# Attention backward loop: attention output two units later, and one VectorE multiply that empties two blocks' accumulators

## The chip, the cores and the metric

The kernel runs on one core of a Trainium2 chip. A core has five engines with queues of their own: TensorE (PE in the profile, with its weight loads as PEld), VectorE (DVE), ScalarE (ACT), GpSimd (POOL) and SyncE (SP). Each runs its instructions in program order and waits on semaphores for what other engines made. Matmuls write PSUM. VectorE and ScalarE empty PSUM in this kernel, and GpSimd works from SBUF to SBUF. The metric is the device time of one launch in microseconds, lower is better.

## The reference

Two attention blocks work on 2048 tokens of width 448, in bf16, and their outputs are concatenated. The kernel computes the outputs and the gradients of all eight inputs for a given `grad_out`. Block A is linear attention. Block B, which the change touches, is attention with 16 heads of width 28 that share one key and one value head:

```python
q = (x @ wq).reshape(B, S, H, Dh).transpose(0, 2, 1, 3)
k = x @ wk
v = x @ wv
scores = einsum("bhqd,bkd->bhqk", q, k) * (Dh ** -0.5)
p = softmax(scores, axis=-1)
o = einsum("bhqk,bkd->bhqd", p, v)
b = o.transpose(0, 2, 1, 3).reshape(B, S, H * Dh) @ wo
```

For block B the backward pass needs, per head and per query, the weighted sum of values o divided by the softmax denominator, the row sum D of dO * o, the gradient of the scores dS = p * (dP - D), and from that dQ = dS k, dK = dS^T q and dV = p^T dO.

## The kernel before

Phase A (about the first 195 us) computes everything of block A, and a short phase projects q, k and v of block B. The rest is one software-pipelined loop over units `u`, from 0 to 539, written out with `tc.manual_schedule()`: each engine executes exactly what the text of the loop issues to it, in that order.

A block `b` (64 of them) is a pair of heads and 256 queries. It takes 8 units, each of which handles 256 keys. Unit `u` belongs to block `u // 8`; "phase" below is `u % 8`. `due(u, lag)` gives the block whose first unit lies `lag` units back, or nothing if `u - lag` is no multiple of 8, so a step with lag 10 runs once per block, at phase 2. In unit `u`:

- `rows_SD` (PE): transposed scores S of unit `u` into two of the three PSUM banks `SB` and dP of unit `w = u - 16` into the two banks `DB`. In odd units the order of the matmuls is S0 S1 D0 D1 S0 S1 D0 D1 (0 and 1 are the heads), in even units S0 S1 D0 S0 S1 D0 D1 D1.
- The third bank of `SB` is `spare` in that unit. `onat_T` and `don_T` (PE transposes) and the output projection use it, and it is the bank that S0 of the next unit writes.
- ACT: `exp` of head 0 (L924), a copy `cp` of dP of head 1 to SBUF (L938), `exp` of head 1 (L970).
- DVE: dS of head 0 (L936, out of PSUM), then what is due of the steps below, and at the end of the unit a 32x32-block transpose of the dS of unit `u - 18` (L1003).
- POOL: dS of head 1 (L939, from `cp`), then what is due. In four of eight blocks it also makes two q staging copies `qst` (L832, phases 6 and 7).
- PE again: odd units do dK (`dk_m`); even units do `o_dq`, which adds two units' share of o (`o_mm`) and of dQ (`dq_mm`) into the bank `oq`, and then the dV groups (`dv_mm`) that are due.

In `oq` the rows 0 to 63 hold o with the softmax denominator of one block, and the rows 64 to 127 hold dQ of an older one. The steps for one block before the change:

| lag (phase) | engine | line | what |
|---|---|---|---|
| 2 to 8 | PE | 656 | `o_mm` into `oq[0:64]` |
| 9 (1) | DVE | 952 | copy of `oq[0:64]` to `oTs[0:64]`, f32 |
| 10 (2) | PE | 790 | `onat_T`: o back to query rows, into `spare` |
| 10 (2) | DVE | 799, 800 | reciprocal of the denominator; normalised o, into `oTs[:, 0:128]` |
| 10 (2) | POOL | 804, 807, 808 | `prod` = dO * o; `don` = dO / denominator; normalised o into `do_nat` in place of dO |
| 12 (4) | DVE, POOL | 812, 813 | `row_D`: row sums of `prod`, into a column of `don` |
| 14 (6) | PE, DVE | 821, 828 | `don_T` into `spare`, copy to `doT` for the dP of units 16 and later |
| 20 to 26 (4, 4, 6, 2) | PE | 656 | `dv_mm`, four groups |
| 27 (3) | DVE | 955 | dQ: `oq[64:128]` times `scale` into `qT_B` as bf16 |

Since `spare` is the next unit's S0 bank, S0 of the next unit waits for the VectorE instruction that reads `spare` last: L800 at phase 2, L828 at phase 6. The normalised o rows leave through a DMA transpose (`oTq`, SP queue, five times) and the output projections in `outs`, of which there is one per block at phase 0.

## Time and profile before

| what | value |
|---|---|
| median of three runs | 1067.29 us (1066.14 to 1067.74) |
| span of the profiled execution | 1064.7 us; its own device time is not listed beside it, the three runs lie 1.4 to 3.0 us above the span |
| loop, first to last `cp` start | 238.7 to 1015.0 us |
| granted TensorE clock | 0.999 |
| busy share of the span | PE 96%, DVE 84%, ACT 82%, POOL 73% |
| busy share from 300 to 400 us | PE 96%, DVE 98%, ACT 99%, POOL 90% |
| L939 POOL dS | 512 times, mean 1156 ns |
| L936 DVE dS, L1003 DVE transpose | 512 times each, mean 667 and 699 ns |
| L924, L938, L970 ACT | 512 times each, mean 612, 617 and 629 ns |
| L952 DVE copy, L955 DVE dQ | 64 times each, median 406 and 427 ns |

Busy times of DVE and ACT contain the overlap of an instruction with the one behind it: the tail of one runs beside the start of the next. For sums the distance from start to start in a stretch without waits is the better number. The three ACT instructions of a unit, for example, start 0.48 us apart where nothing holds them, so ACT needs 1.43 us for a unit.

### The profile page before, as it was taken

Reading aid. Unit: us, or ns where it says so; the run is one execution under the profiler, and the core shown is the slowest. Engines: PE = TensorE matmul, PEld = TensorE weight load, DVE = VectorE, ACT = ScalarE, POOL = GpSimd, SP = SyncE. Lnnn points to the kernel's source line nnn. Section 1 sums busy time; section 2 is a strip of 40 time slices with the busy share of each in tenths; the row PEclk is TensorE's granted clock in tenths of the full one; section 3 lists DMA queues with packets and bytes.
Section 4 is the critical chain, followed back from the end, with each engine's and each line's share of the span. In section 5 each row is a group of like instructions: output and inputs, shape, how many; then the busy total and the mean of one; then the engine's idle time right before and its main releaser. Section 6 shows DMA issues by size and latency. Waiting matters only on the chain.

```text
span 1064.7 us, 40036 instructions
## 1 busy us (share of the span) xinstructions
PE 1023.1 (96%) x16241; PEld 489.1 (46%) x16241; DVE 899.5 (84%) x1797; ACT 870.4 (82%) x1741; POOL 780.7 (73%) x1033
## 2 busy tenths in 40 slices
PE   9999999998999999999999999999999999999998
PEld 5555455434444444444444444444444444444444
DVE  7887400459999999999999999999999999999942
ACT  6463222489999999999999999999999999999522
POOL 6001242218888898899889989988998999888881
PEclk9999999999999999999999999999999999999999
DMA  9849899079999999999999999999999999999963
GB/s 264 167 108 192 171 203 246 22 137 181 193 188 196 182 203 189 188 202 191 197 181 197 181 196 195 193 189 194 196 197 192 199 190 183 208 190 177 222 141 89
DMA packets 689937, 195.15 MB, mean 183 GB/s; under 512 B 670616, under 2 KB 687792, under 8 KB 689752
## 3 DMA queue, kind: packets, MB, share of 16 engines
q1 hardware_dynamic: 680152, 179.92, 99.6%
q0 software_dynamic: 4640, 8.71, 2.9%
q10 hardware_dynamic: 4960, 3.96, 1.3%
q8 instruction: 127, 2.08, 0.8%
q14 instruction: 58, 0.48, 0.2%
HBM read 12.60 MB, written 10.84 MB: 22 GB/s over the span
## 4 chain that ended last, share of the span: by engine, by line
PE 43%; ACT 32%; issue 14%; POOL 5%; DVE 4%; DMA 1%; ACTq 0%; DVEq 0%; POOLq 0%
ACT cp L938 16%; PE agen L81 14%; ACT eT L970 13%; PE agen L656 10%; PE aacc L656 10%; PE aacc L81 5%; POOL dsT L939 3%; PE aacc L790 2%; ACT eT L924 2%; PE aacc L821 1%; DVE dsT L936 1%; DVE dsx L1003 1%; DMA out_dram<-dsT 1%; POOL eT L754 1%; POOL out_dram L778 0%
## 5 line engine op out<-in xcount | busy, mean ns | idle before, releaser
L939 POOL TENSOR_TENSOR dsT<-cp,eT 128x512 bf16<-128x512 bf16 x512 | 587.9, 1156 | 78.9 <-ACT cp L938 71.7
L1003 DVE STREAM_TRANSPOSE dsx<-dsT 128x512 f32<-128x512 f32 x512 | 357.6, 699 | 2.9 <-POOL dsT L939 0.8
L656 PEld LDWEIGHTS <-R 32*128 32x128 bf16 (+1 forms) x9104 | 227.9, 94 | 274.1 <-issue 238.4
L936 DVE TENSOR_TENSOR dsT<-agen,eT 128x512 bf16<-128x512 f32 x512 | 341.7, 667 | 10.9 <-PE agen L656 5.6
L938 ACT ACTIVATE cp<-agen 128x512 bf16<-128x512 f32 x512 | 315.8, 617 | 12.3 <-PE agen L656 11.2
L924 ACT ACTIVATE eT<-aacc 128x512 bf16<-128x512 f32 x512 | 313.6, 612 | 14.8 <-PE agen L656 4.8
L970 ACT ACTIVATE eT<-aacc 128x512 bf16<-128x512 f32 x512 | 322.2, 629 | 0.0
L656 PE MATMUL agen<-dsx,qX 32*32 32x512 bf16 x4096 | 267.6, 375 | 0.0
L656 PE MATMUL agen<-doT,R 32*128 32x256 bf16 x2048 | 247.1, 269 | 3.4 <-DVE dsT L936 1.4
L656 PE MATMUL aacc<-R,R 32*128 32x256 bf16 (+1 forms) x2240 | 218.2, 268 | 7.2 <-DVE oTs L800 2.5
L656 PE MATMUL agen<-eT,R 128*32 128x256 bf16 x2048 | 157.5, 274 | 0.1
L656 PE MATMUL agen<-dsT,R 128*32 128x256 bf16 x2048 | 156.8, 274 | 0.1
L656 PEld LDWEIGHTS <-qX 32*32 32x32 bf16 x4096 | 79.8, 89 | 113.7 <-issue 53.3
L656 PE MATMUL aacc<-eN,don 128*32 128x512 bf16 x1024 | 97.1, 379 | 0.1
L81 PEld LDWEIGHTS <-R 128*128 128x128 bf16 (+1 forms) x517 | 40.8, 98 | 43.5 <-issue 11.5
L406 POOL COPY pk<-R 128x256 bf16<-128x256 bf16 x4 | 1.6, 397 | 73.8 <-DVE R L366 73.7
L81 PE MATMUL agen<-R,R 128*128 128x448 bf16 (+1 forms) x180 | 42.1, 361 | 0.6 <-ACT R L225 0.6
L832 POOL COPY qst<-R 128x512 bf16<-128x512 bf16 x56 | 34.2, 611 | 4.0 <-DMA qX<-qst 3.9
L656 PEld LDWEIGHTS <-don 128*32 128x32 bf16 x1024 | 33.8, 97 | 1.4 <-issue 1.0
L804 POOL TENSOR_TENSOR prod<-R,oTs 128x128 f32<-128x128 bf16 x64 | 27.6, 431 | 9.3 <-DVE oTs L800 9.3
L422 DVE TENSOR_TENSOR osb<-aacc,pr 64x448 bf16<-64x448 f32 x2 | 1.2, 618 | 38.3 <-DMA out_dram<-osb 24.4
L955 DVE TENSOR_SCALAR R<-agen 64x256 bf16<-64x256 f32 x64 | 27.3, 427 | 3.6 <-PE agen L656 1.6
(231 smaller groups left out, 967.8 us busy)
## 6 DMA issues: line engine op xcount, KB each, us to landing
out_dram<-osb ACTq DMA_DIRECT2D x22, 112.0 KB
eN<-eT SPq DMA_TRANSPOSE x128
xa<-in_A_x_dram SPq DMA_DIRECT2D x8, 224.0 KB
ga<-in_grad_out_dram SPq DMA_DIRECT2D x4, 448.0 KB
xa<-in_grad_out_dram POOLq DMA_DIRECT2D x4, 448.0 KB, 6.1
out_dram<-wdq POOLq DMA_DIRECT2D x8, 224.0 KB, 4.0
eT<-in_grad_out_dram SPq DMA_DIRECT2D x4, 448.0 KB
eT<-in_B_x_dram SPq DMA_DIRECT2D x4, 448.0 KB
```

The lines of the kernel that those rows point to most:

```text
L81: nc.tensor.matmul(out_ap, lhsT=lhsT, rhs=rhs, start=start, stop=stop, tile_position=(0, 0))
L656: nc.tensor.matmul(out, lhsT=lhsT, rhs=rhs, start=start, stop=stop, tile_position=pos, skip_group_check=True)
L790: nc.tensor.transpose(onp[:, qb, :, :].rearrange("p h c -> p (h c)"), oTs[0:64, qb * P:(qb + 1) * P], identF[0:64, 0:64], tile_position=(0 ...
L804: nc.gpsimd.tensor_tensor(out=prod[b][:], in0=dnv, in1=os_, op=ALU.mult)
L832: eng.tensor_copy(out=st.rearrange("p (b s) a j -> p b s a j", s=2)[:, :, s, :, :], in_=src.unsqueeze(2).to_broadcast([P, 4, 4, 32]))
L924: nc.scalar.activation(out=eT(u)[:, 0, :], in_=sp[0][:, :], func=ACT.Exp, scale=scale)
L936: nc.vector.tensor_tensor(out=dst[:, 0, :], in0=dp[0][:, :], in1=ew[:, 0, :], op=ALU.mult)
L938: nc.scalar.activation(out=cp[:, :], in_=dp[1][:, :], func=ACT.Copy)
L939: nc.gpsimd.tensor_tensor(out=dst[:, 1, :], in0=cp[:, :], in1=ew[:, 1, :], op=ALU.mult)
L955: nc.vector.tensor_scalar(out=qT_B[g][64 * hp:64 * hp + 64, qc * 256:(qc + 1) * 256], in0=oq[64:128, 0:256], scalar1=scale, scalar2=None, ...
L970: nc.scalar.activation(out=eT(u)[:, 1, :], in_=sp[1][:, :], func=ACT.Exp, scale=scale)
L1003: nc.vector.transpose(out=dsx[b][:, tp, :, :, :].rearrange("p h t c -> p (h t c)").bitcast(F32), in_=dsT[y][:, :, :].rearrange("p h c -> p ...
```

## The change

Seven edits belong together.

1. `o_mm` works on units `u - 4` and `u - 3` instead of `u - 2` and `u - 1`, so o of a block is complete at lag 10 instead of 8, when dQ of the block two earlier is complete as well.
2. One VectorE `tensor_scalar` at phase 3 reads all 128 rows of `oq` and writes `oTs` in f32. Its per-row factor `fac` is 1 for the rows of o and `scale` for the rows of dQ. The row halves of o and dQ swap with the parity of the block. It takes the place of L952 and L955. GpSimd then casts the dQ half of `oTs` to bf16 into `qT_B`. In the last two blocks, where there is no o, dQ is taken as before.
3. `onat_T` and `o_norm` run at lag 12 instead of 10; the normalised o has a tile of its own, `o_s`.
4. `row_D` runs at lag 13 instead of 12, and stands behind L936 on DVE, and before the dS multiply of that unit on GpSimd.
5. The cast of the normalised o into `do_nat` becomes `o_keep`, at lag 14, and the DMA transpose with it.
6. The first `dv_mm` group goes from lag 20 to lag 18; `don` has two buffers instead of three.
7. `identF` shrinks to 64 columns and is copied from `identB`; the output projections from unit 456 on come 8 units later; the one clearing of `oTs` at unit 7 covers 128 rows instead of 64.

```diff
-        identF = pp_.tile([P, P], F32, name="identF", bufs=1)
-        make_identity(nc, identF[:])
+        identF = pp_.tile([P, 64], F32, name="identF", bufs=1)
+        for n in range(2):
+            nc.gpsimd.tensor_copy(out=identF[64 * n:64 * n + 64, :], in_=identB[64 * n:64 * n + 64, 64 * n:64 * n + 64])
         oTs = pp_.tile([P, 256], F32, name="oTs", bufs=1)
+        o_s = pp_.tile([P, 2, 2, 32], F32, name="o_s", bufs=1)
+        fac = pp_.tile([P, 2], F32, name="fac", bufs=1)
...
-        outs.update({456 + 8 * n: (10 + n // 2, n % 2 * (D // 2), (n % 2 + 1) * (D // 2)) for n in range(8)})
+        outs.update({464 + 8 * n: (10 + n // 2, n % 2 * (D // 2), (n % 2 + 1) * (D // 2)) for n in range(8)})
...
         def onat_T(b, bank):
+            r = 64 * (1 - b % 2)
             for qb in range(2):
-                nc.tensor.transpose(onp[:, qb, :, :].rearrange("p h c -> p (h c)"), oTs[0:64, qb * P:(qb + 1) * P],
-                                    identF[0:64, 0:64], tile_position=(0, 0))
+                nc.tensor.transpose(onp[:, qb, :, :].rearrange("p h c -> p (h c)"), oTs[r:r + 64, qb * P:(qb + 1) * P],
+                                    identF[r:r + 64, :], tile_position=(r, 0))
...
         def o_norm(b):
-            os_ = oTs[:, 0:P].rearrange("p (q h c) -> p q h c", q=2, h=2)
+            os_ = o_s[:]
...
-            dn = pw_.tile([P, 2, 2, 32], BF16, name="don", bufs=3)
+            dn = pw_.tile([P, 2, 2, 32], BF16, name="don", bufs=2)
...
-            nc.gpsimd.tensor_copy(out=dnv, in_=os_)
+            o_nat[b] = dnv, os_
+
+        def o_keep(b):
+            nc.gpsimd.tensor_copy(out=o_nat[b][0], in_=o_nat.pop(b)[1])
...
-                if (b := due(u, 10)) is not None:
+                if (b := due(u, 12)) is not None:
                     onat_T(b, spare)
...
                     nc.scalar.activation(out=cp[:, :], in_=dp[1][:, :], func=ACT.Copy)
+                    if (b := due(u, 13)) is not None:
+                        row_D(b)
                     nc.gpsimd.tensor_tensor(out=dst[:, 1, :], in0=cp[:, :], in1=ew[:, 1, :], op=ALU.mult)
...
+                if u % 8 == 3 and 0 <= (b := (u - 11) // 8) < NB + 2:
+                    r = 64 * (1 - b % 2)
+                    rr = slice(r, r + 64) if b < 2 else slice(0, P)
+                    if b < NB:
+                        nc.vector.tensor_scalar(out=oTs[rr, :], in0=oq[rr, 0:256], scalar1=fac[rr, b % 2:b % 2 + 1],
+                                                scalar2=None, op0=ALU.mult)
+                    if b >= 2:
+                        qc, pair, g, hp = blk(b - 2)
+                        rq = slice(64 * hp, 64 * hp + 64)
+                        if b < NB:
+                            nc.gpsimd.tensor_copy(out=qT_B[g][rq, qc * 256:(qc + 1) * 256], in_=oTs[rq, :])
...
                 if (b := due(u, 12)) is not None:
-                    row_D(b)
-                if (b := due(u, 9)) is not None:
-                    nc.vector.tensor_copy(out=oTs[0:64, :], in_=oq[0:64, 0:256])
-                if (b := due(u, 27)) is not None:
-                    qc, pair, g, hp = blk(b)
-                    nc.vector.tensor_scalar(out=qT_B[g][64 * hp:64 * hp + 64, qc * 256:(qc + 1) * 256],
-                                            in0=oq[64:128, 0:256], scalar1=scale, scalar2=None, op0=ALU.mult)
-                if (b := due(u, 10)) is not None:
                     o_norm(b)
+                if (b := due(u, 14)) is not None:
+                    o_keep(b)
...
-                    o_dq((u - 2, u - 1), (u - 20, u - 19))
-                    b, n = divmod(u - 20, 8)
-                    for k in {0: (0, 1), 2: (2,), 6: (3,)}.get(n, ()) if 0 <= b < NB else ():
-                        dv_mm(dv_acc, b, k // 2, k % 2)
+                    o_dq((u - 4, u - 3), (u - 20, u - 19))
+                    for k, lag in enumerate((18, 20, 22, 26)):
+                        if (b := due(u, lag)) is not None:
+                            dv_mm(dv_acc, b, k // 2, k % 2)
```

More of the change, by code (lines that the diff above doesn't have):

```diff
@@ L689 @@
         qst = pp_.tile([P, 8, 4, 32], BF16, name="qst", bufs=1)[:, :, :, :]
-        identF = pp_.tile([P, P], F32, name="identF", bufs=1)
-        make_identity(nc, identF[:])
+        identF = pp_.tile([P, 64], F32, name="identF", bufs=1)
+        for n in range(2):
+            nc.gpsimd.tensor_copy(out=identF[64 * n:64 * n + 64, :], in_=identB[64 * n:64 * n + 64, 64 * n:64 * n + 64])
         oTs = pp_.tile([P, 256], F32, name="oTs", bufs=1)
+        o_s = pp_.tile([P, 2, 2, 32], F32, name="o_s", bufs=1)
+        fac = pp_.tile([P, 2], F32, name="fac", bufs=1)
+        nc.gpsimd.memset(fac[:, :], 1.0)
+        for n in range(2):
+            nc.gpsimd.memset(fac[64 * n:64 * n + 64, n:n + 1], scale)
         wo = pc_.tile([P, 4, D], BF16, name="wo", bufs=1)
@@ L780 @@
         GW = [0, 0, 4, 4, 10, 10, 16, 16, 22, 22, 28, 28, 34, 34, 40, 40, 48, 48, 56, 56, 64, 64]
-        onps, tps2 = {}, {}
+        onps, tps2, o_nat = {}, {}, {}
         def due(u, lag):
@@ L853, in o_mm @@
                 for h in range(2):
-                    mmt(oq[32 * h:32 * h + 32, 0:256], vaug[:, t, :],
-                        eT(v)[:, h, t2 * 256:(t2 + 1) * 256], (0, 32 * h), t == 0, t == 15)
+                    r = 64 * (1 - b % 2) + 32 * h
+                    mmt(oq[r:r + 32, 0:256], vaug[:, t, :],
+                        eT(v)[:, h, t2 * 256:(t2 + 1) * 256], (0, r), t == 0, t == 15)
                 yield
@@ L862, in dq_mm @@
                 for h in range(2):
-                    mmt(oq[64 + 32 * h:96 + 32 * h, 0:256], kn[:, t, :],
-                        dsT[y][:, h, t2 * 256:(t2 + 1) * 256], (0, 64 + 32 * h), t == 0, t == 15)
+                    r = 64 * (b % 2) + 32 * h
+                    mmt(oq[r:r + 32, 0:256], kn[:, t, :],
+                        dsT[y][:, h, t2 * 256:(t2 + 1) * 256], (0, r), t == 0, t == 15)
                 yield
@@ L938 @@
                     nc.scalar.activation(out=cp[:, :], in_=dp[1][:, :], func=ACT.Copy)
+                    if (b := due(u, 13)) is not None:
+                        row_D(b)
                     nc.gpsimd.tensor_tensor(out=dst[:, 1, :], in0=cp[:, :], in1=ew[:, 1, :], op=ALU.mult)
+                if (b := due(u, 13)) is not None and not hasD:
+                    row_D(b)
                 gq, iq = divmod(u % 64 - 30, 8)
@@ L946 @@
                         qc_copy(nc.gpsimd, qst, qq, gq, iq)
-                if (b := due(u, 12)) is not None:
-                    row_D(b)
-                if u == 7:
-                    nc.vector.memset(oTs[64:128, :], 0.0)
-                if (b := due(u, 9)) is not None:
-                    nc.vector.tensor_copy(out=oTs[0:64, :], in_=oq[0:64, 0:256])
-                if (b := due(u, 27)) is not None:
-                    qc, pair, g, hp = blk(b)
-                    nc.vector.tensor_scalar(out=qT_B[g][64 * hp:64 * hp + 64, qc * 256:(qc + 1) * 256],
-                                            in0=oq[64:128, 0:256], scalar1=scale, scalar2=None, op0=ALU.mult)
-                if (b := due(u, 10)) is not None:
+                if u == 7:
+                    nc.vector.memset(oTs[:, :], 0.0)
+                if u % 8 == 3 and 0 <= (b := (u - 11) // 8) < NB + 2:
[9 more added lines that the diff above has]
+                            nc.gpsimd.tensor_copy(out=qT_B[g][rq, qc * 256:(qc + 1) * 256], in_=oTs[rq, :])
+                        else:
+                            nc.vector.tensor_scalar(out=qT_B[g][rq, qc * 256:(qc + 1) * 256], in0=oq[rq, 0:256],
+                                                    scalar1=scale, scalar2=None, op0=ALU.mult)
+                if (b := due(u, 12)) is not None:
                     o_norm(b)
+                if (b := due(u, 14)) is not None:
+                    o_keep(b)
                     if b in (15, 31, 47, 55, 63):
```

## The prediction

> **What bounds the kernel now.** I read the page first, then the sequence of instructions in time, engine by engine, for one ordinary block (units 264 to 271), and last the starts of `cp` (L938) over units 128 to 447, because all three ACT instructions run once per unit and `cp` is the middle one.
>
> ```profile
> span 1064.7 us, 40036 instructions
> PE 1023.1 (96%) x16241; PEld 489.1 (46%) x16241; DVE 899.5 (84%) x1797; ACT 870.4 (82%) x1741; POOL 780.7 (73%) x1033
> L406 POOL COPY pk<-R 128x256 bf16<-128x256 bf16 x4 | 1.6, 397 | 73.8 <-DVE R L366 73.7
> ```
>
> No engine explains the span by its share: shares mix the start, the loop and the tail. The loop is 776 of the 1065 us, and there the time is read from the starts. In the next fence ACT begins at units 264 (two lines), 266, 267; `cp` of 264 starts at 615.81 and of 267 at 620.45.
>
> ```profile
> 615.81 0.65 ACT L938 ACTIVATE cp<-agen 128x512 bf16<-128x512 f32 x1
> 616.28 0.66 ACT L970 ACTIVATE eT<-aacc 128x512 bf16<-128x512 f32 x1
> ...
> 618.75 0.64 ACT L938 ACTIVATE cp<-agen 128x512 bf16<-128x512 f32 x1
> 619.23 0.66 ACT L970 ACTIVATE eT<-aacc 128x512 bf16<-128x512 f32 x1
> 619.96 0.60 ACT L924 ACTIVATE eT<-aacc 128x512 bf16<-128x512 f32 x1
> 620.45 0.59 ACT L938 ACTIVATE cp<-agen 128x512 bf16<-128x512 f32 x1
> ```
>
> The reader is to see the hole: L924 comes 0.73 behind L970 instead of 0.48. Write cp(p) for the start of `cp` at phase p. Medians from cp(p) to the next, p = 0 to 7: 1.51, 1.43, 1.70, 1.43, 1.61 or 1.50 by the block's parity, 1.43, 1.50 or 1.54, 1.43. So odd phases go at ACT's own pace, and even ones reach 1.50 at best (S0's second half stands behind D1, which waits for the previous `cp`). A block takes 12.02 or 11.97, mean 12.00; four times 2.93 would be 11.72. The excess sits at phase 2 (0.20) and, small, at 4. DVE shows why:
>
> ```profile
> 616.87 0.69 DVE L936 TENSOR_TENSOR dsT<-agen,eT 128x512 bf16<-128x512 f32 x1 [0.24 <-PE agen L656]
> 617.48 0.41 DVE L952 COPY oTs<-agen 64x256 f32<-64x256 f32 x1
> 617.81 0.69 DVE L1003 STREAM_TRANSPOSE dsx<-dsT 128x512 f32<-128x512 f32 x1
> 618.43 0.65 DVE L936 TENSOR_TENSOR dsT<-agen,eT 128x512 bf16<-128x512 f32 x1
> 619.01 0.16 DVE L799 RECIPROCAL rl<-aacc 128x4 f32<-128x4 f32 x1
> 619.20 0.29 DVE L800 TENSOR_TENSOR oTs<-aacc,rl 128x128 f32<-128x128 f32 x1
> ...
> 622.41 0.27 DVE L812 TENSOR_REDUCE Dq<-prod 128x4 f32<-128x128 f32 x1
> 622.60 0.70 DVE L1003 STREAM_TRANSPOSE dsx<-dsT 128x512 f32<-128x512 f32 x1
> 623.23 0.65 DVE L936 TENSOR_TENSOR dsT<-agen,eT 128x512 bf16<-128x512 f32 x1
> ...
> 624.42 0.65 DVE L936 TENSOR_TENSOR dsT<-agen,eT 128x512 bf16<-128x512 f32 x1
> 625.10 0.29 DVE L828 COPY doT<-aacc 64x256 bf16<-64x256 bf16 x1
> ```
>
> Here is a chain from cp(0) at 615.81: L936 of phase 1 starts 1.06 later (PE's D0 stands behind that `cp`); then start to start 0.61, 0.33 (L952 to L1003), 0.62, 0.58, 0.19 to L800; that takes 0.29; 0.47 from its end to L924 of phase 3 (PE writes S0 into the freed bank); 0.49 to `cp`. The sum is 4.64, and 620.45 - 615.81 is 4.64. The chain is complete, so DVE's order before L800 sets the time, with nothing to spare. POOL has slack:
>
> ```profile
> 619.47 1.16 POOL L939 TENSOR_TENSOR dsT<-cp,eT 128x512 bf16<-128x512 bf16 x1 [0.32 <-ACT cp L938]
> 620.58 0.43 POOL L804 TENSOR_TENSOR prod<-R,oTs 128x128 f32<-128x128 bf16 x1
> 620.97 0.40 POOL L807 TENSOR_TENSOR don<-R,rl 128x128 bf16<-128x128 bf16 x1
> 621.44 0.29 POOL L808 CAST R<-oTs 128x128 bf16<-128x128 f32 x1
> ```
>
> L939 starts 0.72 behind its `cp` and `prod` 1.11 behind L939: `prod` ends at 621.01, 0.56 after cp(3). Its reader, L812, comes only at 622.41.
>
> **The change part by part.**
>
> *The two copies become one.* DVE loses one instruction per block, 0.33 to 0.40 from start to start. But the copy that remains stands at phase 3, L936, L1003, L936, reciprocal, multiply follow it, and the bank is freed at phase 4: the chain of 4.64 moves from cp(0)..cp(3) to cp(2)..cp(5) and does not get shorter. Bounds for the new instruction: like L952 (0.61 before it, 0.33 behind) or like L955 (620.03, 620.72, 621.07: 0.69 and 0.35). I take L952, whose output is f32 too, and keep 0.10 for the range. The Trainium skill, "VectorE: DVE Perf Modes", section "Two Vector instructions with no wait between them", models an instruction as held until all earlier ones finished when its input or output starts in another 32-partition group; that would fit L955's 0.69, and the new copy starts at row 0. By the rule the step costs 4.64, by the L955 row 4.74; the sum below is the same for both, as a longer chain decides.
>
> *Phase 2 is relieved*: it has no normalisation any more, and two `dv_mm` groups come to it, as phase 4 has now. Without DVE's delay that phase takes 1.50 (the better parity), so cp(2) to cp(4) falls from 3.13 to 2.93: a gain of 0.20. Bound: 1.61, a gain of 0.09.
>
> *`row_D` at lag 13 adds a wait.* It now stands on DVE behind L936 of phase 5, one unit after `prod` was issued, where it was two. From cp(4): L939 0.72 later, `prod` 1.11 behind it, 0.43 long, so done at 2.26. DVE meanwhile: cp(5) is at 1.71 (2.93 + 1.71 = 4.64), L936 starts about 0.41 before it, as at phase 3 now, and 0.61 behind that, at 1.91, DVE stands at the reduction. It waits 0.44: 0.35 for `prod` and 0.09 for the semaphore (L800 ended 231.26 and L804 started at 231.35, in the one place where POOL was idle; between 0 and 0.2 for the range). Queued behind it are L1003, L936 of phase 6, the `doT` copy, and with that copy S0 of phase 7 and ACT. The chain from cp(4): 0.72 + 1.11 + 0.43 + 0.09 = 2.35; reduction to L1003 0.19; 0.63 to L936; 0.58 (the other parity) or 0.68 (as above) to the copy; 0.28 long; 0.47 to L924; 0.49 to `cp`: cp(7) at 4.99 or 5.09, mean 5.04. Now cp(4) to cp(7) is 4.47 or 4.54, mean 4.50. A loss of 0.54. The copy's chain, 1.71 + 1.43 + 1.50 = 4.64, lies inside it.
>
> *The GpSimd cast of dQ.* No row shows 64x256 bf16 from f32. Nearest are L406 (256 elements, bf16, 397 ns), L808 (f32 to bf16, 128 elements, 289) and L832 (512 elements, 611). I take 0.40, some 0.36 from start to start. It stands between L939 of phase 3 and L939 of phase 4: cp(3) + 0.67 + 1.11 + 0.36 = cp(3) + 2.14, or cp(4) + 0.71, against cp(4) + 0.72 when `cp` allows the next one. It just fits; at 0.29 it costs nothing either, at 0.61 it adds 0.20 to the chain. The Trainium skill, "GPSIMD Engine Reference", section "Performance versus the Vector engine", speaks against moving it: elementwise work is about twice as slow there. The L406 row (397 ns) against L955 (427 ns) does not show that at this size. By the page, my estimate is 0.85, and the sum would rise by 0.45 a block, some 27 us.
>
> *The rest of POOL's queue.* `row_D`'s small multiply now goes ahead of L939 of phase 5, which starts 0.48 late; each unit gives back 0.32. With `o_keep` (0.25, moved from phase 3 to 6), the staging copies (0.57 each) and the store's issue (0.6) in the blocks that have them, my count of lateness is 0.16 at phase 6, 0.27 at 7, 0.52 at 0, at most 0.70 at 1, 0.38 at 2, none at 3: the next chain starts clean. PE's `don_T` waits for that multiply, about 0.1 longer than now; S0 of phase 7 waits for DVE longer, so it costs nothing (without that cover 0.1).
>
> *With one answer, nothing:* `o_mm` later (same matmuls beside `dq_mm`); `don` with two buffers (last read at lag 26, rewritten at 28); `o_s`; the DMA transpose on SP four units later (3.2 us, its first projection is due ten units, 15 us, later). The new constants replace 0.74 us of POOL before the loop by five short instructions: 0, within -0.7 and +0.5. The wider clearing at unit 7 is 0.27 with DVE idle on both sides: 0. The last projections, 8 units later, put one more into the drain, where PE is the limit: +0.4 (its row is 0.57 for 16 matmuls, and it may be 0).
>
> **Sum.** Block now 3.13 + 4.50 + 4.37 = 12.00. After 2.93 + 5.04 + 4.37 = 12.34. The 0.34 falls on about 60 of 64 blocks (the first four are slower already by the projection of dO, the last drains): 20.2 us, and 0.4 at the end. The span goes from 1064.7 to 1085.3. The median lies 2.6 above the profiled span, so the median becomes about 1087.9; I say 1087.
>
> **Rivals.**
> 1. *Faster: DVE was the bound, and its lost 0.33 to 0.48 shortens every block.* For it: DVE is busy 98% in the loop. Against: the chain of 4.64 keeps all its links. With it and everything else at the floor a block takes 11.72 + 0.21 = 11.93: 4 us less, 1063. Without it at most 0.28 x 60 = 17 less, 1050. It decides if `prod` is ready when DVE comes to the reduction: 0.44 earlier than I count.
> 2. *No chain over `prod`, the copy like L955*: cp(2) to cp(5) 4.64 to 4.74, rest as now: 11.97 to 12.11, between -2 and +7 us; 1065 to 1074.
> 3. *POOL becomes the bound*: the cast costs 0.61 or the lateness does not fall to zero at phase 3, so that `prod` is 0.2 to 0.4 later in every block: 12 to 24 us more, 1099 to 1111.
>
> **How the numbers follow.** My case 0.66; rival 1 0.09; rival 2 0.12; rival 3 0.13. My case alone spans 1079 (no semaphore time, the shorter copy in both parities: 0.14 a block less) to 1100 (0.20 for the semaphore, phase 2 at 1.61: 0.22 more). The range 1068 to 1102 leaves out rival 1, part of rival 2 and most of rival 3. About 0.2% (2 us) can be told from no change: faster 0.09, same 0.06 (half of rival 2), slower 0.85.
>
> **What would show it.** Right: the reduction at phase 5 preceded by some 0.4 us of idle DVE released by `prod`; cp(6) to cp(7) about 1.8; cp(2) to cp(3) 1.50; the cast near 0.40 and L939 of phase 4 still 0.72 behind `cp`. Wrong: no gap at the reduction (rival 1 or 2), L939 of phase 4 late (rival 3), or phase 2 still above 1.6.

## The result and the profile after

The changed kernel takes 1089.8 us (median of four runs, 1089.33 to 1090.82) against 1066.72 us (four runs, 1064.92 to 1067.74) for the kernel before: a ratio of 1.0218, with a 95% interval of 1.0204 to 1.0233. It is slower by 23 us. The forecast was 1087, range 1068 to 1102.

The first lines of the page of after and the first line of its chain of waits, then that line of the chain in the page of before:

```profile
span 1087.8 us, 40152 instructions
PE 1022.9 (94%) x16232; PEld 482.7 (44%) x16241; DVE 882.4 (81%) x1735; ACT 872.8 (80%) x1741; POOL 802.3 (74%) x1098
PE 40%; POOL 22%; ACT 14%; DVE 12%; issue 11%; DMA 1%; ACTq 0%; DVEq 0%; POOLq 0%; SPq 0%
```
```profile
PE 43%; ACT 32%; issue 14%; POOL 5%; DVE 4%; DMA 1%; ACTq 0%; DVEq 0%; POOLq 0%
```

PE has the same busy time as before (1023 us). DVE, which the change relieves, lost 17 us of busy time (899.5 to 882.4) and 62 instructions. The span grew all the same. The chain that ends last now runs through POOL for 22% of the span (5% before) and through ACT for only 14% (32% before): ACT waits more often for others.

The profiled execution has a span of 1087.8 us and a device time of 1089.5 us. From the first to the last `cp` the loop took 797.9 us instead of 776.3, so 21.6 of the 23.1 us between the spans lie in it. 1.6 lie before it, and the tail is 0.1 shorter. In the 13 profiles of this study the first `cp` starts between 238.0 and 240.5 us, in kernels that all have the same text for the first phase. The first L406 row, at 75 us, is already 1.6 later in after than in before (76.58 against 75.01), and nothing that the change edits comes ahead of it. So the 1.6 is scatter of the first phase, and the length of the loop compares two kernels better than the span does. It comes from one profile of each kernel, and runs of one kernel lie some us apart (twelve runs of v6: 1064.04 to 1068.58), so a difference of 2 or 3 us between two loops counts only where the steps show it too. The table gives it for each kernel, with the medians of the even steps cp(p) to cp(p+1) over units 128 to 447 (cp(p) is the start of `cp` at phase p). Odd steps are 1.43 throughout, unless a text below says otherwise. Two values with a stroke stand for the two parities of the block; in v8 the value before "or" is that of the blocks whose predecessor has no q staging copies.

| kernel | loop, us | phase 0 | phase 2 | phase 4 | phase 6 | mean block |
|---|---|---|---|---|---|---|
| before | 776.3 | 1.50 | 1.70 | 1.61 / 1.50 | 1.50 / 1.54 | 12.03 |
| after | 797.9 | 1.50 | 1.51 | 1.77 | 1.95 / 1.87 | 12.42 |
| e1 sum of `o_s` | 785.3 | 1.50 | 1.51 | 1.77 | 1.79 / 1.57 | 12.21 |
| e2 no cast | 791.4 | 1.50 | 1.51 | 1.77 | 1.73 / 1.86 | 12.30 |
| e5 cast at phase 1 | 793.2 | 1.50 | 1.51 | 1.77 | 1.73 / 1.87 | 12.34 |
| e3 product first | 790.6 | 1.50 | 1.51 | 1.77 | 1.80 / 1.73 | 12.29 |
| e4 `row_D` alone | 811.9 | 1.51 | 1.70 | 2.25 / 2.13 | 1.50 | 12.66 |
| v1 multiply at phase 2 | 791.9 | 1.50 | 1.51 | 1.67 | 1.83 / 1.96 | 12.33 |
| v2 both | 781.8 | 1.50 | 1.51 | 1.67 | 1.69 | 12.14 |
| v4 `don_T` at lag 15 | 786.2 | 1.46 | 1.51 | 1.67 | 1.50 | 12.24 |
| v6 sums at phase 4 | 775.4 | 1.51 | 1.51 | 1.67 | 1.50 | 12.04 |
| v9 stores by SP | 775.8 | 1.51 | 1.51 | 1.67 | 1.50 | 12.06 |
| v8 cast on DVE | 789.3 | 1.51 | 1.51 or 2.04 / 2.17 | 1.68 | 1.50 | 12.31 |

Before and after differ at three phases: 0.19 gained at phase 2, some 0.21 lost at phase 4, some 0.39 lost at phase 6. The sequence of DVE instructions of after, in one block in which o belongs to an even block number (cp(4) at 633.52, cp(5) at 635.29, cp(6) at 636.72, cp(7) at 638.59):

```profile
632.25 0.47 DVE L969 TENSOR_SCALAR oTs<-agen,fac 128x256 f32<-128x256 f32 x1
632.64 0.70 DVE L1027 STREAM_TRANSPOSE dsx<-dsT 128x512 f32<-128x512 f32 x1
633.27 0.65 DVE L948 TENSOR_TENSOR dsT<-agen,eT 128x512 bf16<-128x512 f32 x1
633.85 0.17 DVE L806 RECIPROCAL rl<-aacc 128x4 f32<-128x4 f32 x1
634.05 0.29 DVE L807 TENSOR_TENSOR o_s<-aacc,rl 128x128 f32<-128x128 f32 x1
634.25 0.70 DVE L1027 STREAM_TRANSPOSE dsx<-dsT 128x512 f32<-128x512 f32 x1
634.88 0.66 DVE L948 TENSOR_TENSOR dsT<-agen,eT 128x512 bf16<-128x512 f32 x1
635.83 0.29 DVE L822 TENSOR_REDUCE Dq<-prod 128x4 f32<-128x128 f32 x1 [0.29 <-POOL prod L811]
636.03 0.70 DVE L1027 STREAM_TRANSPOSE dsx<-dsT 128x512 f32<-128x512 f32 x1
636.66 0.65 DVE L948 TENSOR_TENSOR dsT<-agen,eT 128x512 bf16<-128x512 f32 x1
637.34 0.29 DVE L838 COPY doT<-aacc 64x256 bf16<-64x256 bf16 x1
```

POOL in the same block:

```profile
632.78 1.16 POOL L953 TENSOR_TENSOR dsT<-cp,eT 128x512 bf16<-128x512 bf16 x1 [0.32 <-ACT cp L950]
633.87 0.39 POOL L975 CAST R<-oTs 64x256 bf16<-64x256 f32 x1
634.25 1.16 POOL L953 TENSOR_TENSOR dsT<-cp,eT 128x512 bf16<-128x512 bf16 x1
635.36 0.43 POOL L811 TENSOR_TENSOR prod<-R,o_s 128x128 f32<-128x128 bf16 x1
635.75 0.40 POOL L814 TENSOR_TENSOR don<-R,rl 128x128 bf16<-128x128 bf16 x1
636.26 0.22 POOL L823 TENSOR_TENSOR don<-Dq,rl 128x4 bf16<-128x4 f32 x1
```

The reader is to see that `o_s` is finished at 634.34, but that `prod` starts only at 635.36: POOL executes in order, and the dS multiply of 1.16 us (634.25) lies in between. The row sums (L822), on the other side, stand one unit behind `o_s` in DVE's order. DVE reaches them at about 635.5, is idle for 0.29, and with it the transpose, the next dS and the `doT` copy (L838) come late. That copy frees the bank that S0 of phase 7 needs. On ACT the hole of before at phase 2 (0.73 from L970 to L924) has closed, and one stands at phase 6: L994 at 637.20, L936 at 638.10, which is 0.90 instead of 0.48.

```profile
637.20 0.65 ACT L994 ACTIVATE eT<-aacc 128x512 bf16<-128x512 f32 x1
638.10 0.60 ACT L936 ACTIVATE eT<-aacc 128x512 bf16<-128x512 f32 x1 [0.25 <-PE agen L656]
638.59 0.59 ACT L950 ACTIVATE cp<-agen 128x512 bf16<-128x512 f32 x1
```

The waits from 300 to 980 us (total, times, longest) have one of 0.4 us on DVE in each of 55 blocks (the second line):

```profile
PEld L831 <- POOL don L823: 34.1, 55, 1.0
DVE Dq L822 <- POOL prod L811: 22.3, 55, 0.6
```

The first line is the longer one: PE's `don_T` (L831) waits for POOL's small multiply (L823). It does not end last in this kernel, since the `doT` copy (L838), which reads what `don_T` writes, follows L948 on DVE in every block without an idle time of its own that the waits would list.

In the blocks of the other parity the gap is longer. POOL's line of the cast and DVE's line of the reduction in such a block, with cp(4) at 645.89:

```profile
645.14 1.16 POOL L953 TENSOR_TENSOR dsT<-cp,eT 128x512 bf16<-128x512 bf16 x1 [0.32 <-DVE oTs L969]
646.36 0.40 POOL L975 CAST R<-oTs 64x256 bf16<-64x256 f32 x1
646.84 1.15 POOL L953 TENSOR_TENSOR dsT<-cp,eT 128x512 bf16<-128x512 bf16 x1
```
```profile
648.41 0.29 DVE L822 TENSOR_REDUCE Dq<-prod 128x4 f32<-128x128 f32 x1 [0.52 <-POOL prod L811]
649.82 0.27 DVE L838 COPY doT<-aacc 64x256 bf16<-64x256 bf16 x1
```

Here the cast begins 1.22 behind the dS multiply instead of 1.09, and the next multiply 0.48 behind the cast instead of 0.38. That multiply starts 0.95 behind its `cp` instead of 0.73 in the first block. (The releaser that the first line names, L969, belongs to the wait of the cast behind it; L953 of phase 3 starts 0.68 behind its `cp` in both parities.) In 31 of the 62 casts, those that work on rows 64 to 127, POOL's queue has a semaphore wait ahead of the cast. In the trace these casts wait for the semaphore of POOL's own previous instruction as well as for DVE, and the multiply behind each waits for the cast as well as for `cp`; the other 31 have no wait of that kind:

```profile
L975 POOL CAST R<-oTs x62: 386/394/409, 260.4 to 1019.5; 64x256 bf16<-64x256 f32 x62
L975 POOLq EVENT_SEMAPHORE  x31: 17/17/17, 271.7 to 1018.6; - x31
```

The cast itself takes 394 ns (the row gives the shortest, the median and the longest).

### The profile page after: what moved, and what is told of

The parts are those of the page before. It is cut to its first block, busy times and chain, and to the rows that moved or that the text cites. A ratio compares the mean times of both kernels' runs of the same rounds, so it can differ in the third digit from the quotient of the medians.

```text
span 1087.8 us, 40152 instructions
## 1 busy us (share of the span) xinstructions
PE 1022.9 (94%) x16232; PEld 482.7 (44%) x16241; DVE 882.4 (81%) x1735; ACT 872.8 (80%) x1741; POOL 802.3 (74%) x1098
## 4 chain that ended last, share of the span: by engine, by line
PE 40%; POOL 22%; ACT 14%; DVE 12%; issue 11%; DMA 1%; ACTq 0%; DVEq 0%; POOLq 0%; SPq 0%
POOL dsT L953 16%; PE agen L81 14%; PE agen L656 11%; PE aacc L656 9%; ACT cp L950 8%; PE aacc L81 6%; ACT eT L994 5%; DVE dsx L1027 3%; DVE dsT L948 2%; POOL prod L811 2%; POOL R L975 2%; DVE doT L838 1%; DVE oTs L969 1%; DVE Dq L822 1%; ACT eT L936 1%
## 5 line engine op out<-in xcount | busy, mean ns | idle before, releaser
L953 POOL TENSOR_TENSOR dsT<-cp,eT 128x512 bf16<-128x512 bf16 x512 | 587.9, 1157 | 75.4 <-ACT cp L950 59.4
L948 DVE TENSOR_TENSOR dsT<-agen,eT 128x512 bf16<-128x512 f32 x512 | 343.3, 671 | 25.9 <-PE agen L656 20.7
L656 PEld LDWEIGHTS <-R 128*32 128x32 bf16 (+1 forms) x9104 | 224.9, 94 | 286.6 <-issue 238.5
L936 ACT ACTIVATE eT<-aacc 128x512 bf16<-128x512 f32 x512 | 313.6, 612 | 34.0 <-PE agen L656 20.9
L994 ACT ACTIVATE eT<-aacc 128x512 bf16<-128x512 f32 x512 | 322.3, 629 | 0.0
L656 PE MATMUL agen<-doT,R 32*128 32x256 bf16 x2048 | 259.8, 270 | 2.6 <-DVE dsT L948 1.1
L406 POOL COPY pk<-R 128x256 bf16<-128x256 bf16 x4 | 1.6, 397 | 75.3 <-DVE R L366 75.2
L822 DVE TENSOR_REDUCE Dq<-prod 128x4 f32<-128x128 f32 x64 | 18.3, 286 | 25.3 <-POOL prod L811 25.2
L831 PE MATMUL aacc<-identB,don 128*32 128x128 bf16 x256 | 18.5, 224 | 21.3 <-POOL don L823 20.3
L811 POOL TENSOR_TENSOR prod<-R,o_s 128x128 f32<-128x128 bf16 x64 | 27.7, 433 | 10.8 <-DVE o_s L807 10.8
```

The lines of the kernel that those rows point to most:

```text
L656: nc.tensor.matmul(out, lhsT=lhsT, rhs=rhs, start=start, stop=stop, tile_position=pos, skip_group_check=True)
L811: nc.gpsimd.tensor_tensor(out=prod[b][:], in0=dnv, in1=os_, op=ALU.mult)
L822: nc.vector.tensor_reduce(out=Dq[:, :, :, 0], in_=prod[b][:], axis=AX.X, op=ALU.add)
L936: nc.scalar.activation(out=eT(u)[:, 0, :], in_=sp[0][:, :], func=ACT.Exp, scale=scale)
L948: nc.vector.tensor_tensor(out=dst[:, 0, :], in0=dp[0][:, :], in1=ew[:, 0, :], op=ALU.mult)
L953: nc.gpsimd.tensor_tensor(out=dst[:, 1, :], in0=cp[:, :], in1=ew[:, 1, :], op=ALU.mult)
```

## The experiments

My theory was that 0.4 us or more of every block is the wait of the row sums for a product that POOL makes too late, and that the rest is the chain of the accumulator, which is only moved. The rivals were that POOL is overloaded by the cast, and that the cost lies in the fused multiply.

**e1: the row sums without the product.** Everything stays, except that the reduction reads `o_s`, which DVE itself made, so that it has nothing to wait for.

```diff
-            nc.vector.tensor_reduce(out=Dq[:, :, :, 0], in_=prod[b][:], axis=AX.X, op=ALU.add)
+            nc.vector.tensor_reduce(out=Dq[:, :, :, 0], in_=o_s[:], axis=AX.X, op=ALU.add)
```

> The changed kernel, but the row sums of phase 5 are taken of the normalised o, which VectorE itself made a unit earlier, and not of the product dO*o, which GpSimd makes. The product is still computed and not used, so D and all gradients behind it are not those of the reference; the same instructions stand on every engine in the same order, only the wait of VectorE for the product is gone. Theory (the wait of the reduction for the product costs the time): the reduction starts where VectorE comes to it, the next limit is TensorE's don transpose behind GpSimd's small multiply, cp(4) to cp(7) falls from 5.07 and 5.15 us by about 0.36 and 0.22, 60 blocks: about 17 us less, 1073 us (1067 to 1078). Rival (GpSimd's extra cast and its fuller queue cost the time): both are still there, 1086 to 1091. Rival (the later normalisation or the fused multiply cost the time): 1086 to 1091.

Measured: 1075.57 us (1075.43 to 1077.63), ratio 1.0074 (1.005 to 1.0099). The loop is 12.6 us shorter than that of after. In the sequence of DVE the gap is gone, and a small one stands at the `doT` copy instead:

```profile
639.08 0.66 DVE L948 TENSOR_TENSOR dsT<-agen,eT 128x512 bf16<-128x512 f32 x1
639.66 0.27 DVE L822 TENSOR_REDUCE Dq<-o_s 128x4 f32<-128x128 f32 x1
639.85 0.70 DVE L1027 STREAM_TRANSPOSE dsx<-dsT 128x512 f32<-128x512 f32 x1
640.48 0.65 DVE L948 TENSOR_TENSOR dsT<-agen,eT 128x512 bf16<-128x512 f32 x1
641.32 0.28 DVE L838 COPY doT<-aacc 64x256 bf16<-64x256 bf16 x1 [0.20 <-PE aacc L831]
```

So the wait is worth 12.6 of the 21.6 us by which the loop grew. It is not worth all of it, since the next limit lies close behind: the small multiply (L823) ends late on POOL, and PE's `don_T` (L831), which reads what it wrote, starts 0.05 behind that end, at cp(6) in the block shown and at cp(6) - 0.22 in the other parity. The loss that remains in e1 is that and phase 4, at 1.77.

**e2: without the cast.** dQ is not cast into `qT_B`.

```diff
-                        if b < NB:
-                            nc.gpsimd.tensor_copy(out=qT_B[g][rq, qc * 256:(qc + 1) * 256], in_=oTs[rq, :])
-                        else:
+                        if b >= NB:
```

> The changed kernel without GpSimd's cast of dQ: dQ of the first 62 blocks is left out of qT_B, so the gradients of x and wq of block B are not computed. Theory (the chain over the product sets the time; the cast only matters where it delays the dS multiply of phase 4): blocks whose cast writes rows 0 to 63 are unchanged (5.07 us from cp(4) to cp(7), the dS multiply starts 0.72 behind cp(4) anyway), in the others that start falls from 0.95 to 0.72, which is 0.2 us in 30 blocks: 5 to 6 us less, 1084 us (1081 to 1087). Rival (GpSimd is the bound): its queue loses 0.38 to 0.6 us in every block, 23 to 36 us less, 1054 to 1067.

Measured: 1081.49 us (1081.04 to 1084.39), ratio 1.013 (1.0107 to 1.0152); the loop is 6.5 us shorter than that of after. The dS multiply of phase 4 starts at cp(4) + 0.72 in all blocks, and phase 6 falls by 0.22 in that parity in which the multiply started at cp(4) + 0.95 (1.95 to 1.73), not in the other (1.87 to 1.86). So the cast costs nothing by its 0.39, and 0.22 by the waits in half of the blocks. That the cast makes POOL the bound is out: 15 us of the loss remain without it.

**e5: the cast at phase 1.** The cast of dQ runs six units later, in a phase that does not lead to `prod`.

```diff
+                if (b := due(u, 33)) is not None and b < NB - 2:
+                    qc, pair, g, hp = blk(b)
+                    rq = slice(64 * hp, 64 * hp + 64)
+                    nc.gpsimd.tensor_copy(out=qT_B[g][rq, qc * 256:(qc + 1) * 256], in_=oTs[rq, :])
```

> The changed kernel with GpSimd's cast of dQ six units later, at phase 1, where GpSimd idles 0.3 us in each unit. Theory: as without the cast, the dS multiply of phase 4 starts 0.72 us behind cp(4) in all blocks, the longer half of the blocks loses 0.2 us: 5 us less, 1084 to 1085 us (1081 to 1088). Rival (GpSimd is the bound): the load is the same, 1088 to 1091.

Measured: 1084.06 us (1083.62 to 1084.69), ratio 1.0149 (1.013 to 1.0167), loop 4.7 us shorter than that of after, with the same steps as e2 (1.73 and 1.87). Most of what e2 saves (6.5 us) is therefore the place of the cast and not its work; the 1.8 us between the two runs no step explains.

**e3: the product first.** At phase 4 the reciprocal, the normalisation and `prod` are issued ahead of POOL's dS multiply; `don` stays behind it.

```diff
+                    if (b := due(u, 12)) is not None:
+                        o_norm(b)
                     nc.gpsimd.tensor_tensor(out=dst[:, 1, :], in0=cp[:, :], in1=ew[:, 1, :], op=ALU.mult)
...
                 if (b := due(u, 12)) is not None:
-                    o_norm(b)
+                    if not hasD:
+                        o_norm(b)
+                    o_don(b)
```

> The changed kernel with GpSimd's product dO*o of phase 4 issued ahead of that unit's dS multiply, everything else in place. Theory (wait for the product): the product is done about 1.3 us behind cp(4) and not 2.3 to 2.5, VectorE finds it ready at 1.97 and does not wait; the dS multiply of phase 4 starts 0.5 us later, which nobody waits for; don and the small multiply end at 2.9 to 3.0, TensorE's don transpose follows them, cp(4) to cp(7) becomes 4.8 to 4.9 instead of 5.07 and 5.15: 0.26 us in 60 blocks, 15 us less, 1074 us (1069 to 1079). Rival (GpSimd is the bound): same work in its queue, 1086 to 1091, or slower.

Measured: 1082.70 us (1080.64 to 1082.77), ratio 1.0131 (1.011 to 1.0151): 8 us more than I expected. The reduction does not wait any more (cp(5) + 0.16), but POOL's order is now `prod`, dS, `don`, small multiply, in the sequence of POOL:

```profile
631.00 0.43 POOL L811 TENSOR_TENSOR prod<-R,o_s 128x128 f32<-128x128 bf16 x1 [0.15 <-DVE o_s L807]
631.39 1.15 POOL L958 TENSOR_TENSOR dsT<-cp,eT 128x512 bf16<-128x512 bf16 x1
632.50 0.40 POOL L818 TENSOR_TENSOR don<-R,rl 128x128 bf16<-128x128 bf16 x1
632.99 0.21 POOL L826 TENSOR_TENSOR don<-Dq,rl 128x4 bf16<-128x4 f32 x1
```

The small multiply (L826) writes into `don`, and it starts 0.08 after `don` has ended, so it ends at cp(6) - 0.05 or - 0.11 in the medians, and `don_T` starts another 0.05 later. I had put this path at 0.1 less and had not counted that e1 and e3 meet the same limit: what POOL gives back at the reduction it owes at `don_T`.

**e4: `row_D` alone.** The kernel before, with `row_D` at lag 11 instead of 12 and placed as in the change; nothing else is changed.

```diff
+                    if (b := due(u, 11)) is not None:
+                        row_D(b)
                     nc.gpsimd.tensor_tensor(out=dst[:, 1, :], in0=cp[:, :], in1=ew[:, 1, :], op=ALU.mult)
...
-                if (b := due(u, 12)) is not None:
-                    row_D(b)
```

> The kernel before, with one part of the change alone: row_D one unit earlier (lag 11 instead of 12, one unit behind the product as in the changed kernel), behind VectorE's dS multiply and ahead of GpSimd's; two copies out of PSUM, o and the normalisation where they were, no cast on GpSimd. Theory (a reduction one unit behind the product waits for it): at phase 3 VectorE stands at the reduction 0.20 us behind cp(3), the product is done at 0.57 to 0.61; it waits 0.4, the dQ copy of that unit, the transpose and the dS multiply of phase 4 come 0.36 later than now, and D0 of phase 5 with them: 0.3 us in 60 blocks, 18 us more than the kernel before, 1085 us (1077 to 1092). Rival (the cast, the later normalisation or the fused copy cost the time): within 2 us of the kernel before.

Measured: 1102.89 us (1102.37 to 1104.21), ratio 1.0339 (1.0321 to 1.0357). One step moved by one unit costs 35.6 us in the loop by itself, which is more than the whole change. The direction is as expected, the size twice as large. The sequence of DVE at the place (cp(3) lies between the first two lines):

```profile
650.86 0.66 DVE L936 TENSOR_TENSOR dsT<-agen,eT 128x512 bf16<-128x512 f32 x1
651.88 0.28 DVE L812 TENSOR_REDUCE Dq<-prod 128x4 f32<-128x128 f32 x1 [0.35 <-POOL prod L804]
652.19 0.43 DVE L957 TENSOR_SCALAR R<-agen 64x256 bf16<-64x256 f32 x1
```

Behind the reduction stands not only a transpose but also the dQ eviction (L957, L955 in the kernel before). It starts when the reduction has ended, and PE's next group into that bank waits for it (20.7 us in 52 blocks from 300 to 980 us). Phase 4 goes from 1.61 and 1.50 to 2.25 and 2.13. My expectation had the dQ eviction in the queue, but counted only the later dS multiplies behind it and not PE's group that needs the bank. So e4 shows that a reduction one unit behind `prod` waits (0.35 here); its price, 35.6 us, comes in large part (the 20.7 us of PE's waits) by a path through the bank `oq`, which the changed kernel does not have, as no eviction stands behind its reduction.

**v1: the multiply at phase 2.** The fused multiply and the cast move one phase earlier, behind `o_dq` in the text, so that the chain to the bank at phase 4 is shorter.

```diff
-                if u % 8 == 3 and 0 <= (b := (u - 11) // 8) < NB + 2:
+                    if u % 8 == 2 and 0 <= (b := (u - 10) // 8) < NB + 2:
```

> The changed kernel with the one multiply out of PSUM right behind the matmuls that complete o and dQ (phase 2, ahead of that unit's transpose) instead of at phase 3, and GpSimd's cast behind the dS multiply of phase 2. Theory (from cp(4) to cp(7) the chain over the product decides, whatever the normalisation gains): cp(4) to cp(5) falls from 1.77 to about 1.53, but the reduction still waits until 2.30 behind cp(4), so cp(7) stays 4.97 to 5.07 behind cp(4); only the cast's delay in half the blocks goes: 1083 us (1080 to 1086). Rival (the chain over the copy and the normalisation decides): 0.24 in 60 blocks, 14 us less, 1075 us.

Measured: 1083.86 us (1082.79 to 1084.86), ratio 1.0159 (1.0138 to 1.018). The time is the expected one. Phase 4 falls from 1.77 to 1.67 (I had put 1.53), but from cp(4) to cp(7) the kernel takes 4.93 and 5.06, exactly as e2 does with a phase 4 of 1.77 (1.77 + 1.43 + 1.73, and 1.77 + 1.43 + 1.86). What v1 gains is what e2 and e5 gain: with the cast one unit earlier, the dS multiply of phase 4 starts at cp(4) + 0.72 in all blocks. The shorter phase 4 itself gives nothing, because the chain over `prod` counts from cp(4) and passes cp(5) by. The 1.67 is a floor of its own: PE's `onat_T` starts at cp(4) - 0.28, since it waits for the `exp` that reads the bank, and reciprocal and multiply follow it up to cp(4) + 0.67. The reciprocal starts 0.66 behind the dS multiply here and 0.58 in after, so in v1 it waits for `onat_T` and in after for DVE's own order. Before's 1.70 at phase 2 stood almost on it.

**v2: both.** v1 and e3 together.

> Both: the multiply out of PSUM at phase 2, and the product ahead of the dS multiply of phase 4 on GpSimd. Theory: the product no longer makes VectorE wait, the earlier normalisation counts now; phase 4 takes 1.53, phase 6 still 1.75, because TensorE's don transpose waits for GpSimd's small multiply, as with the product first alone. cp(4) to cp(7) 4.71, block 12.01, about the kernel before: 1067 us (1062 to 1072). If the two gains did not add, it stays at 1080 to 1083.

Measured: 1074.23 us (1072.77 to 1074.58), ratio 1.0066 (1.0048 to 1.0083): 2 us above the range. The loop is 16.1 us shorter than that of after, 2.8 more than v1 (6.0) and e3 (7.3) give together. The steps show it too: from cp(4) to cp(7) v2 takes 4.79, 0.32 less than after, where v1 takes 0.12 less and e3 0.15. With the chain over `prod` gone, the shorter phase 4 counts. Phase 6 is 1.69; the small multiply ends at cp(6) - 0.15 there and `don_T` starts 0.05 later.

**v4: `don_T` later as well.** v2, with `don_T` and its copy at lag 15 instead of 14.

```diff
-                if (b := due(u, 14)) is not None:
+                if (b := due(u, 15)) is not None:
                     don_T(b, spare)
```

> As the run before it, and the don transpose and the doT copy at lag 15 instead of 14, so at phase 7, where nothing else uses the spare bank, behind dK's matmuls. Theory: the wait of TensorE for the small multiply and the copy that S0 of phase 7 waits for are gone from phase 6; all even phases come near 1.50 to 1.53, block 11.76, 0.24 less than the kernel before in 62 blocks: 1052 us (1048 to 1060). If doT arrives late for the dP matmuls of the next unit, phase 7 grows by 0.1 to 0.3 and the time is 1058 to 1070.

Measured: 1076.26 us (1075.51 to 1077.28), ratio 1.0088 (1.0071 to 1.0105). Missed: phase 6 falls to 1.50, but phase 7, an odd one, rises from 1.43 to 1.79. The late `doT` that I had named as the risk is not the cause. One such unit, with cp(7) at 643.82, by engine (L834 is `don_T`, the 16 matmuls are dK's, L841 is the `doT` copy):

```profile
642.80 0.65 ACT L987 ACTIVATE eT<-aacc 128x512 bf16<-128x512 f32 x1
643.49 0.29 PE L834 MATMUL aacc<-identB,don 128*32 128x128 bf16 x4
643.71 1.05 PE L656 MATMUL agen<-dsx,qX 32*32 32x512 bf16 x16
643.97 0.27 DVE L841 COPY doT<-aacc 64x256 bf16<-64x256 bf16 x1
644.70 0.29 PE L656 MATMUL agen<-doT,R 32*128 32x256 bf16 x2
```

The copy is done at 644.24, and dP of the next unit starts 0.46 later. PE is what is late: `don_T` stands ahead of dK in the text of the loop, not behind it as I had expected, and waits for the `exp` (L987) that reads the spare bank. So dK starts at cp(7) - 0.11 in the medians, where it starts at cp(7) - 0.59 in v2, and S0 of the next unit behind it at cp(7) + 0.87 instead of + 0.39. The wait changed its place.

**v6: product, `don` and row sums all at phase 4.** v2, with POOL's `prod`, `don` and small multiply ahead of its dS multiply, and on DVE the transpose and then the reduction in the same unit; `don_T` at lag 14.

```diff
                     if (b := due(u, 12)) is not None:
                         o_norm(b)
+                        o_don(b)
+                        to_dsx(u - 18)
+                        row_D(b)
                     nc.gpsimd.tensor_tensor(out=dst[:, 1, :], in0=cp[:, :], in1=ew[:, 1, :], op=ALU.mult)
```

> The multiply out of PSUM at phase 2 as in the second run of the last set, and at phase 4 on GpSimd, ahead of that unit's dS multiply, the product, don and the small multiply; on VectorE the row sums at phase 4 too, behind that unit's transpose and ahead of the dS multiply of phase 5; don transpose at lag 14. Theory: the product is done at 1.18 behind cp(4) and VectorE comes to the reduction at 1.20, so that it waits little; the small multiply ends at about 1.9 instead of 2.95, TensorE's don transpose at phase 6 waits for nothing of it and phase 6 falls from 1.69 to 1.50; phase 4 keeps 1.67, which is the way from the exp of the unit before over the transpose and the normalisation to S0 and is there in the kernel before too (1.70). Block 11.9, 0.1 less than the kernel before: 1061 us (1057 to 1066). If the dS multiply of phase 4, now a unit's length late on GpSimd, makes VectorE or TensorE wait, phases 5 to 7 grow and the time is 1066 to 1085.

Measured: 1066.06 us (twelve runs, 1064.04 to 1068.58), ratio 0.9981 (0.9968 to 0.9994). It is 0.2% faster than the kernel before, just at the bound of what can be told, and 2.2% faster than the changed one; I had expected 1061. The sequence of DVE at phase 4:

```profile
633.94 0.29 DVE L807 TENSOR_TENSOR o_s<-aacc,rl 128x128 f32<-128x128 f32 x1
634.15 0.70 DVE L924 STREAM_TRANSPOSE dsx<-dsT 128x512 f32<-128x512 f32 x1
634.78 0.29 DVE L825 TENSOR_REDUCE Dq<-prod 128x4 f32<-128x128 f32 x1
634.98 0.68 DVE L960 TENSOR_TENSOR dsT<-agen,eT 128x512 bf16<-128x512 f32 x1
```

The transpose covers the time that `prod` needs (634.31 to 634.74 on POOL in this block), and no wait is left in it; from 300 to 980 us ten blocks still have one (4.2 us in all, 22.3 in after). Of the 40 blocks of units 128 to 447, 28 take 11.90, as expected. The mean is 12.04, because ten blocks with staging copies, or right behind one, take 12.2 to 13. My reading is that POOL, whose dS multiply now comes behind three small instructions, has no slack left for the copies and for the store's issue; v9 tests the store.

**v9: stores by SP.** v6, with the stores of the first output issued by SP instead of POOL.

```diff
-                nc.gpsimd.dma_start(out0[i * P:(i + 1) * P, D:2 * D], ots[i])
+                nc.sync.dma_start(out0[i * P:(i + 1) * P, D:2 * D], ots[i])
```

> As the run with the row sums at phase 4, and the stores of the output rows issued by SyncE instead of GpSimd (each takes GpSimd 0.6 us). In the run before, 11.90 was the time of most blocks, but blocks with q staging copies and a store on GpSimd took 12.1 to 13.0, because the dS multiply ran up to 2.3 us behind its cp. Theory (there GpSimd is the bound): without the stores the five blocks per staging group at 12.2 fall to about 11.9, 3 to 4 us less than that run, 1062 us (1059 to 1066). If SyncE's queue holds the stores or the transposes behind them, nothing is gained: 1066 to 1070.

Measured: 1065.88 us (twelve runs, 1063.52 to 1068.45), ratio 0.9987 (0.9975 to 1.0), not to be told from v6 and 4 us above what I expected: the loop is 775.8 against 775.4. Five of the six blocks that took 12.2 fell to 11.90, so the store was what made these long. But two blocks of 13.5 and 13.6 came; in the first of them a staging copy on POOL waits for its DMA:

```profile
495.25 0.61 POOL L845 COPY qst<-R 128x512 bf16<-128x512 bf16 x1 [1.86 <-DMA qX<-qst]
```

What makes that DMA late in some blocks was not settled.

**v8: the cast on DVE.** v9, with the cast of dQ on DVE at phase 1, to unload POOL.

```diff
+                if (b := due(u, 33)) is not None and b < NB - 2:
...
+                    nc.vector.tensor_copy(out=qT_B[g][rq, qc * 256:(qc + 1) * 256], in_=oTs[rq, :])
```

> As the run beside it, and the cast of dQ on VectorE at phase 1 instead of on GpSimd behind phase 2. Theory: GpSimd loses another 0.4 us a block, so its lateness in the staging blocks does not build up; VectorE has 0.2 us free in phases 7, 0 and 1. Nearly all blocks at 11.90, 6 to 8 us less than the run with the row sums at phase 4: 1059 us (1055 to 1063). If VectorE has no room at phase 1, phase 2 grows by 0.1 to 0.2 and the time is 1063 to 1072.

Measured: 1080.10 us (five runs, 1078.43 to 1081.46), ratio 1.0119 (1.0102 to 1.0137), 21 us above what I expected. The blocks fall into two kinds. Of the 20 blocks of units 128 to 447 whose predecessor has no q staging copies, 16 take 11.90, as expected. In the 20 that follow a block with staging copies, phase 2 takes 2.04 or 2.17 (1.51 elsewhere, with two exceptions) and phase 3 1.57 (1.43 elsewhere), and the block 12.6 or 12.76. In just these 20 blocks the cast takes over 1.1 us, as the last section shows.

## Why the prediction was right, point by point

- **The wait of the row sums for `prod`.** This was the named step, and it holds. The profile has 55 waits of DVE on L811 with 22.3 us in all from 300 to 980 us, e1 takes them away and the loop gets 12.6 us shorter. e4 makes such a wait alone; there the loop gets 35.6 us longer, but in large part by the bank behind it. The predicted idle time was 0.44; it is 0.29 in the first block shown and 0.52 in the second, 0.41 in the mean (22.3 / 55). The semaphore's part was put at 0.09 and takes 0.03 (`prod` ends at 635.79 and L822 starts at 635.83 in the block shown). I had read the 0.09 from POOL waiting for DVE, where it holds (0.08 in v6, v2 and v8 wherever `prod` waits for `o_s`), and used it for DVE waiting for POOL.
- **The chain from cp(4) to cp(7).** Predicted 4.99 or 5.09 by parity, measured 5.15 or 5.07. The 5.09 is the one in which the `doT` copy is held behind L948 (0.68 from start to start, 0.58 in the other parity), as the Trainium skill's "VectorE: DVE Perf Modes", "Two Vector instructions with no wait between them", models it: in that parity the copy reads and writes from row 64, and the instructions ahead of it from row 0. The parity predicted at 4.99 came out 0.16 higher: its cast and the multiply behind it wait for POOL's own previous instruction, so that the dS multiply of phase 4 starts 0.23 late. My sentence "it just fits" held in the other half of the blocks only; I had counted the durations of POOL's instructions and not the waits that a queue keeps on its own engine. e2 and e5 price this at 5 to 7 us. As a sign of being right I had named cp(6) to cp(7) at about 1.8; my own terms give 1.90 (5.04 less 1.71 and 1.43), and 1.95 and 1.87 are measured.
- **The two copies become one.** I took L952's 0.33 from start to start and kept 0.10 for the range. The fused multiply needs 0.39 (632.25 to 632.64), and phase 4 came out at 1.77 instead of 1.71. It costs nothing, as I had written, because the longer chain over `prod` decides from cp(4) to cp(7): v1 takes 0.10 out of phase 4 and needs the same time over these three units as e2, which does not. In e1, where that chain is gone, the 1.77 remains as a loss.
- **Phase 2.** Predicted 1.50, measured 1.51. The gain of 0.19 is there.
- **The cast.** Predicted 0.40, measured 0.394. The estimate of 0.85 that the prediction works out from the "GPSIMD Engine Reference" of the Trainium skill is not what this instruction takes.
- **`don_T` behind the small multiply.** I let it cost nothing because S0 of phase 7 waits longer for DVE. In after that is so. e1 and e3 show how thin the cover is: without the wait at the reduction, `don_T` is the limit, and phase 6 falls by 0.16 or 0.30 in e1, not by the whole 0.4.
- **The sum.** I took a block of 4.37 + 2.93 + 5.04 = 12.34 after the change. Its three parts measure 4.36, 2.94 and 5.11 (the mean of 5.07 and 5.15), so the term that was too small is the chain over `prod`, by 0.07, and within it the cast's own wait: 0.23 in half of the blocks is 0.12, of which the semaphore takes back 0.06. The mean block is 0.39 longer (12.42 less 12.03), where I had 0.34 on 60 blocks, 20.2 us (20.4 by the rounded 0.34). An ordinary block is 0.39 or 0.43 longer by parity; blocks that were slower in before already are lengthened less or not at all, and all 64 together make the 21.6 us of the loop. The drain was put at +0.4 and is -0.1. So the span, forecast at 1085.3 and measured at 1087.8, is missed by 1.4 in the loop and 1.6 of scatter in the first phase, less 0.5 in the drain. That it came so near is in part luck: the cast's wait, which I had not counted, and the semaphore, which I had counted too long, offset each other by half.
- **The rivals.** That DVE was the bound (rival 1) falls: it was relieved of 17 us, the kernel got slower, and DVE now stands idle at the reduction. That there is no chain over `prod` (rival 2) falls by the same gap. That POOL is the bound (rival 3) was right in its mechanism for half of the blocks, with L953 of phase 4 late by 0.23, but the cast was not long, and the lateness at phase 3 is gone in each block.

## What to carry to other kernels

A step on one in-order queue that reads what another in-order queue makes has two prices: how old the data is when the step's turn comes, and what is queued behind the step. e4 moved a 0.28 us reduction by one unit and cost 36 us, because its producer stood behind a 1.16 us instruction and a bank's eviction stood behind the reduction. Taking instructions off an engine that is 98% busy gained nothing here as long as the chain through it kept its links. What turned 2.2% slower into 0.2% faster was to move the producer with its reader: v6, with product, `don` and row sums in one unit, and the multiply out of PSUM one unit earlier (v1), which alone gave 6 us.
